# Transformer block on one core: query and output projections in five packed groups, fourteen score blocks a pass on VectorE

## Chip, core and metric

The kernel runs on one core of a Trainium2 chip. The metric is the device time of one execution in microseconds, and the median over runs. The core has five engines with a queue of instructions each, worked off in order: TensorE (PE, with its weight loads PEld), VectorE (DVE), ScalarE (ACT), GpSimd (POOL) and SyncE (SP), which here issues most DMAs. Results of TensorE lie in PSUM, eight banks of 512 f32 values on each of 128 partitions; everything else lies in SBUF.

## What is computed

A transformer block before normalisation: attention of 32 query heads with one shared key and value head of width 20, then a gated FFN, each with a residual. S = 2048 tokens, D = 640, Df = 1536, bf16.

```python
x = A_x
xn = layernorm(x)
q = (xn @ wq).reshape(B, S, 32, 20).transpose(0, 2, 1, 3)
k, v = xn @ wk, xn @ wv
p = softmax(einsum("bhqd,bkd->bhqk", q, k) * 20 ** -0.5)
h = x + einsum("bhqk,bkd->bhqd", p, v).transpose(0, 2, 1, 3).reshape(B, S, 640) @ wo
g, u = layernorm(h) @ w_gate, layernorm(h) @ w_up
out = h + (gelu(g) * u) @ w_down
```

## The kernel before

**Padded heads.** A head is 20 wide and takes 32 rows: four heads fill 128 partitions (rows 0 to 19, 32 to 51, 64 to 83, 96 to 115; the twelve rows after each are zero). 32 heads are NG = 8 groups. wq is widened into wq_pad (L323, L449, L462 to L465), wo into wo_pad (L327, cleared L1166, loaded by four DMAs L1169). q stands in qT (L331) in two slots of 512 tokens (a chunk), made by q_proj (L585): per chunk and group five matmuls over D, and one cast by VectorE (L608). The first chunk is made by q_proj_first (tile 0) and a q_proj over tiles 1 to 3.

**Attention in blocks.** There are 16 tiles of 128 tokens with two halves each, four groups (16 heads) to a half; a tile's half is a pass. A pass has 64 blocks (16 key tiles x 4 head rows). For a block one matmul (qk_mm, L665) on 32 rows gives 128 keys by 512 scores; four blocks on different rows run side by side. Five blocks make a cycle: three in banks 0 to 2, two in banks 3 and 4, and ACT takes the exponential of each set in one instruction (L743) into one of three buffers pbuf. PV (L811) multiplies each block with the values on 32 columns, four heads side by side, into one bank that collects the pass.

**Blocks on VectorE.** Some blocks of a pass (D_UNITS = 12; the first pass none, the last two D_LAST = 8) are not given to ACT: stream_d (L669) puts their scores into an aux bank, VectorE writes them as integers (L699), which read as bf16 approximate a power of two, and shifts two more copies per pair of blocks (L708); PV then takes three weighted terms of each such block (values v_w, scaled for the last ND_KT = 3 key tiles). With 12 such blocks a pass has 52 left for ACT.

**After a pass**, normalise (L830) transposes, divides and transposes back (L837, L842, L849) into onT. After both halves of a tile, wo_proj (L894) multiplies onT with wo_pad, eight matmuls of 512 columns and eight of 128 (L906), and VectorE adds to xh (L913). Then come the second layer norm, a transpose by DMA (L507), the FFN (L942 to L985, tanh on ACT L975), its down projection (L1001) and the store (L1012). The last tile has its own function (last_tile, L1016).

**Order.** A planner in the code (_Sched, L41 to L276) gives each task a duration, dependences, a priority and slots of buffers, plays them through (schedule, L94) and so fixes the order on every engine; semaphore waits (resolve, L225) keep it correct. Score matmuls of the stream go ahead of other TensorE tasks when these would delay them by more than a spare time (L140 to L152). A DMA holds SP's queue for 0.08 us in the plan and ends after its given duration (L187); a task waiting for it adds HOP (0.12 for SP) and its lag (0.3 for side work on TensorE). Side work is what is neither scores nor PV: projections and FFN. It shares two aux banks (5 and 7, AUX_pool) with the scores of VectorE's blocks.

A second plan in the program, "with_maximum", runs only if a sum of the softmax falls outside a range; it doesn't run here.

Of the kernel before, what the change touches and what calls it, by code (L numbers as in the profile page):

```python
# [10 lines left out]
P = 128  # L11
# [13 lines left out]
class _Pool:  # L25
    def __init__(self, n):
        self.free_at = [0.0] * n
        self.users = [[] for _ in range(n)]
        self.busy = [False] * n

# [4 lines left out]
class _Task:  # L35
    __slots__ = ("eng", "fn", "dur", "deps", "prio", "acq", "rel", "dma", "name", "start", "end", "seq",
                 "extra", "sem", "val", "needed", "know", "pos", "lag", "cfg", "after", "paced", "opens", "rides",
                 "groups", "late", "spare")


class _Sched:  # L41
# [13 lines left out]
    SPARE_A, SPARE_B = .28, .7  # L55

# [10 lines left out]
    def add(self, eng, fn, dur, deps=(), prio=0.0, acq=(), rel=(), dma=None, name="", lag=0.0,  # L67
# [7 lines left out]
        t.spare = None  # L75
        t.after = list(after)
# [17 lines left out]
    def schedule(self):  # L94
# [8 lines left out]
        cfg = None  # L103
# [19 lines left out]
        while left:  # L123
            best = None
            for e in self.ENGINES:
                cands = []
                for at, t in ready[e]:
                    if t.rides and not (cfg == t.cfg and at <= free[e] + 0.02 and t.rides() - groups):
                        at += self.PATIENCE
                    if t.paced and paced:  # L130
                        at = max(at, paced_at - self.AHEAD)
                    for s in t.acq:
                        p = s.pool
                        open_ = [f for f, b in zip(p.free_at, p.busy) if not b]
                        if not open_:
                            break
                        at = max(at, min(open_))
                    else:
                        cands.append((max(at, free[e]), t))
# [16 lines left out]
                pick = min((c for c in cands if c[0] <= t0 + 1e-9), key=lambda c: (c[1].prio, c[1].seq))  # L156
# [5 lines left out]
            if e == "pe" and opened is not None and not (t.cfg is None and at - free[e] < self.GAP):  # L162
# [11 lines left out]
            for s in t.acq:  # L174
# [3 lines left out]
                p.busy[i] = True  # L178
                t.extra += p.users[i]
# [9 lines left out]
            else:  # L189
# [16 lines left out]
                if e == "pe" and t.cfg is None:  # L206
                    whole = t.end
                    paced_at = max(paced_at, at) + dur / self.SHARE
# [70 lines left out]
def bass_sequential_preLN__grouped_kv_mqa__glu_gated_geglu__prompt_kernel(  # L279
# [31 lines left out]

    sc = _Sched()
# [10 lines left out]
    wq_pad = sb("wq_pad", [P, ND, H, 32])  # L323
# [3 lines left out]
    wo_pad = sb("wo_pad", [P, NG, D])  # L327
# [32 lines left out]
    ND_KT = 3  # L360
    v_w = sb("v_w", [P, 3, ND_KT, 32])
    wq_sb = dbuf[:].rearrange("p a b n -> p (a b n)")[:, 0:ND * D].rearrange("p (c n) -> p c n", c=ND)
# [86 lines left out]
    z_wq = sc.add("pool", lambda e: e.memset(wq_pad[:, :, :, Dh:32], 0.0), 2.0, prio=nprio(), name="z_wq")  # L449
# [11 lines left out]
    for h in range(2):  # L461
        wq_c.append(sc.add("act", (lambda h: lambda e: e.activation(  # L462
            wq_pad[:, :, 16 * h:16 * h + 16, 0:Dh],
            wq_sb.rearrange("p c (h n) -> p c h n", h=H)[:, :, 16 * h:16 * h + 16, :], ACT.Copy))(h),
            d_act(1600), [dma_wq, z_wq], prio=nprio(), name=f"wqpad{h}"))  # L465

    def wq_l(cc, g):
        return wq_pad[:, cc, 4 * g:4 * g + 4, :].rearrange("p a b -> p (a b)")
# [90 lines left out]

    def q_proj_first(h, sl, bk, eng):  # L560
        pr = nprio()

        def part(g0):
            def fn(e):
                ins = None
                for g in range(g0, g0 + 2):
                    for cc in range(ND):
                        ins = e.matmul(bk()[:, g * P:(g + 1) * P], wq_l(cc, 4 * h + g),
# [3 lines left out]
        a = sc.add("pe", part(0), 0.65, ln1_T[0] + [wq_c[h]], prio=pr, acq=[sl], name=f"q0a_{h}")  # L572
        b = sc.add("pe", part(2), 0.65, [a], prio=pr, name=f"q0b_{h}")
        o = qT[:, 0, 4 * h:4 * h + 4, 0:P]

        def ev(e):
            i = bk().rearrange("p (g n) -> p g n", g=4)
            return e.activation(o, i, ACT.Copy) if eng == "act" else e.tensor_copy(o, i)
        q_ready[(0, h)] = [sc.add(eng, ev, d_act(512) if eng == "act" else d_ps(512), [b], prio=pr, rel=[sl],
                                  name=f"q0e_{h}")]  # L580
        xnT_readers[0].append(b)

    last_qk = {}

    def q_proj(c, g, t0, t1):  # L585
# [12 lines left out]
        deps = [x for t in range(t0, t1) for x in ln1_T[t]] + [wq_c[g // 4]] + xnT_readers[NT - 1][:1]  # L598
# [6 lines left out]
        for t in range(t0, t1):  # L605
            xnT_readers[t].append(d)
        o = qT[:, c % 2, g, (t0 % 4) * P:(t0 % 4) * P + n]
# [3 lines left out]
        for t in range(t0, t1):  # L611
            q_ready.setdefault((t, g // 4), []).append(ev)

# [7 lines left out]
    D_UNITS, D_LAST = 12, 8  # L621
# [38 lines left out]
    state = {"pv": None, "ont": None, "qk": None}  # L660
# [8 lines left out]
    def stream_d(n, which):  # L669
# [11 lines left out]
        def choose(task, used):  # L681
# [5 lines left out]
            if u[3] in used:  # L687
# [3 lines left out]
                      prio=HOT + 4 * n + (1 if which else 0.5), acq=[ax] + ([d_sl] if half == 0 else []),  # L691
                      name=f"qkd_{n}", cfg="row", rides=lambda: {u[3] for u in left})
        qk_t.late = choose
        last_qk[(t, h)] = qk_t
# [60 lines left out]
    def pv(n, t, h, part, exps, p_sl):  # L755
# [60 lines left out]
        pv_t.late = choose  # L816
        if n == in_pass[(t, h)][1]:
# [76 lines left out]
    def wo_proj(t, ont):  # L894
        deps0 = [onorm[(t, 0)], onorm[(t, 1)]] + wo_ready
        done = []
        for c0, c1 in ((0, 512), (512, D)):
# [3 lines left out]
            step = 1 if c0 == 0 else 4  # L901
            for g0 in range(0, NG, step):
                def fn(e, g0=g0, c0=c0, c1=c1, step=step, bk=bk):
                    ins = None
                    for g in range(g0, g0 + step):
                        ins = e.matmul(bk()[:, 0:c1 - c0], onT[:, ont.index, g, :], wo_pad[:, g, c0:c1],  # L906
                                       start=(g == 0), stop=(g == NG - 1))
                    return ins
                lastp = g0 + step == NG
                prev = sc.add("pe", fn, 0.215 if c0 == 0 else 0.2225, deps0 if prev is None else [prev], prio=pr,  # L910
# [8 lines left out]
    def ffn(t0, t1):  # L919
# [6 lines left out]
        for tri in range(NF // (3 * k)):  # L926
            gsl = G_pool.slot()
            ges, zts, uts, first_g = [], [], [], []
            for j in range(3):
# [26 lines left out]
                gm, pr = job(wg_sb, dma_wg, "g", acq + [ax], [], bk)  # L956
                ge = sc.add("dve", lambda e, gsl=gsl, col=col, bk=bk: e.tensor_copy(g_gs[:, gsl.index, col], bk()),  # L957
# [10 lines left out]
                um, pr = job(wu_sb, dma_wu, "u", [ax], [], bk)  # L968
                uts.append(sc.add("dve", lambda e, gsl=gsl, col=col, bk=bk: e.scalar_tensor_tensor(  # L969
# [10 lines left out]
            for j in range(3):  # L980
# [7 lines left out]
                    [ths[j], uts[j]], prio=pr, acq=acq, rel=[gsl], after=hh_all[:1], name=f"hh{t0}_{fc0}"))  # L988
# [26 lines left out]

    def last_tile(t, ont):  # L1016
# [15 lines left out]
        def wo_part(j, c0, c1, g0):  # L1032
            def fn(e):
                ins = None
                for g in range(g0, g0 + 4):
                    ins = e.matmul(acc(j), onT[:, ont.index, g, :], wo_pad[:, g, c0:c1], start=False, stop=(g == NG - 1))
# [3 lines left out]
        for j, c0, c1 in halves_:  # L1040
            r = add("pe", wo_part(j, c0, c1, 0), 0.56, [r, onorm[(t, 0)]] + wo_ready, name=f"wa{j}_{t}")
# [124 lines left out]
    z_wo = sc.add("pool", lambda e: e.memset(wo_pad[:], 0.0), 4.5, [ln1_nm[NT - 1]], prio=nprio(), name="z_wo")  # L1166
    wo_ready = []
    for hl in range(4):
        wo_ready.append(load("sp", wo_pad[32 * hl:32 * hl + Dh, :, :],  # L1169
                             A_wo.rearrange("(g l d) n -> l d g n", g=NG, l=4)[hl], f"wo{hl}", 6.0,  # L1170
                             [z_wo] + after_T))
# [10 lines left out]
    for t in range(NT):  # L1182
# [11 lines left out]
        if t % 4 == 0 and t + 4 < NT:  # L1194
# [3 lines left out]
            for g in range(NG):  # L1198
                q_proj(t // 4 + 1, g, t + 4, t + 8)
            counter[0] = max(keep, counter[0])  # L1200
        ffn(t, t + 1)

# [46 lines left out]
    with nc.body("with_maximum"):  # L1249
# [6 lines left out]
        wo_ready, outs = [], []  # L1256
# [37 lines left out]
        for t in range(NT):  # L1294
# [5 lines left out]
            for h in range(2):  # L1300
                ax, bk = aux()

                def q_all(e, h=h, t=t, bk=bk):
                    ins = None
                    for g in range(4):
                        for cc in range(ND):
                            ins = e.matmul(bk()[:, g * P:(g + 1) * P], wq_l(cc, 4 * h + g),
# [4 lines left out]
                q_done.append(sc.add("dve", lambda e, h=h, bk=bk: e.tensor_copy(  # L1312
                    qT[:, 0, 4 * h:4 * h + 4, 0:P], bk().rearrange("p (g n) -> p g n", g=4)), 0.7, [a], prio=nprio(),
                    rel=[ax], name=f"ge{t}_{h}"))
# [55 lines left out]
```

## Time and profile before

| | us |
|---|---|
| runs | 834.09, 835.21, 835.84 (median 835.21) |
| the profiled execution | 833.07 |
| its span, first to last instruction | 831.0 |
| first exponential (L743) starts | 14.6 |
| last exponential starts | 806.1 |
| landing of a transpose xnT<-xn_tmp, median | 2.6 |
| landing of a store out_dram<-xh, median | 1.8 |

Busy slices of the span, 40 equal ones, in tenths (9 is 90% or more):

```
PE   4898999999999999999999999999999999999997
DVE  7567878888788877987787798878888788777762
ACT  5899999999999999999999999999999999999991
POOL 6500001001001111011000011111101011011010
```

A matmul's listed time is its length from start to end; consecutive ones overlap, so the busy time of a group is less than count times length. Lines of a group read: line, engine, operation, out<-in with partitions x elements, xcount, then busy us, mean ns of one, and the engine's idle time before them with what ended it. Some matmul records are missing (L594 should have 120 of 512 columns, L906 120).

### The profile page before, as it was taken

The page shows a single profiled execution, that of the slowest core. Times are in us where ns is not written, and L with a number is a line of the kernel's source. Part 1 is how long each engine was busy: PE and PEld are TensorE (multiplying, and loading weights), DVE is VectorE, ACT ScalarE, POOL GpSimd, SP SyncE. Part 2 cuts the span into 40 slices and gives each one's busy share as a digit, 9 for nine tenths or more (in the row PEclk, how much of TensorE's full clock was granted, in tenths as well). Part 3 has the DMA queues.
Part 4 walks back from the last instruction along what each step waited for, and adds up shares of the span by engine and source line. Part 5 has one row for each costly group of instructions (what it writes and reads, how often), then busy time and mean ns, then how long its engine had stood idle before and what let it go on. Part 6 is the DMA issues. An engine that isn't in the chain of part 4 may idle for free.

```text
span 831.0 us, 17917 instructions
## 1 busy us (share of the span) xinstructions
PE 767.0 (92%) x7743; PEld 303.9 (37%) x7800; DVE 648.7 (78%) x1320; ACT 799.6 (96%) x740; POOL 92.4 (11%) x157
## 2 busy tenths in 40 slices
PE   4898999999999999999999999999999999999997
PEld 3322233333234343333323343343434333334345
DVE  7567878888788877987787798878888788777762
ACT  5899999999999999999999999999999999999991
POOL 6500001001001111011000011111101011011010
PEclk9899999999999999999999999999999999999999
DMA  8680000000000000000000000000000000000000
GB/s 215 113 285 1 10 1 9 1 10 9 1 9 10 9 9 2 17 2 17 1 9 10 1 10 9 9 9 10 10 1 17 9 9 2 17 2 9 17 1 20
DMA packets 30347, 18.94 MB, mean 23 GB/s; under 512 B 21944, under 2 KB 28984, under 8 KB 30264
## 3 DMA queue, kind: packets, MB, share of 16 engines
q1 hardware_dynamic: 28808, 17.54, 8.2%
q8 instruction: 62, 1.02, 0.5%
q10 hardware_dynamic: 1456, 0.22, 0.2%
q14 instruction: 21, 0.17, 0.1%
HBM read 10.21 MB, written 2.62 MB: 15 GB/s over the span
## 4 chain that ended last, share of the span: by engine, by line
ACT 85%; PE 9%; DVE 4%; DMA 1%; issue 0%; SPq 0%
ACT pbuf L743 83%; PE ps L665 3%; ACT g_z L975 2%; PE ps L811 2%; PE ps L942 1%; DVE dbuf L699 1%; PE ps L1106 1%; DVE dbuf L708 1%; PE ps L1001 1%; DMA xh<-in_A_x_dram 1%; DVE hhT L985 1%; DMA xnT<-xn_tmp 1%; PE ps L1115 0%; ACT kT L551 0%; PE ps L906 0%
## 5 line engine op out<-in xcount | busy, mean ns | idle before, releaser
L743 ACT ACTIVATE pbuf<-ps 128x1536 bf16<-128x1536 f32 (+1 forms) x674 | 766.8, 1334 | 4.4 <-PE ps L665 4.0
L665 PE MATMUL ps<-qT,kT 32*128 32x512 bf16 x2048 | 289.0, 386 | 38.4 <-ACT pbuf L743 24.8
L699 DVE TENSOR_SCALAR dbuf<-ps 128x512 int16<-128x512 f32 x364 | 247.0, 683 | 88.2 <-PE ps L665 85.8
L811 PE MATMUL ps<-pbuf,v_ext 128*32 128x512 bf16 x1684 | 210.4, 389 | 1.0 <-DVE oT L837 0.5
L811 PE MATMUL ps<-dbuf,v_w 128*32 128x512 bf16 x1092 | 161.2, 380 | 0.0
L665 PEld LDWEIGHTS ps<-qT,kT 32*128 32x128 bf16 x2048 | 73.8, 91 | 226.9 <-ACT pbuf L743 165.7
L708 DVE TENSOR_SCALAR dbuf<-dbuf 128x1024 int16<-128x1024 int16 x364 | 145.2, 433 | 2.7
L960 POOL TENSOR_TENSOR g_z<-g_gs 128x512 bf16<-128x512 bf16 x45 | 49.2, 1092 | 423.6 <-DVE g_gs L957 423.6
L942 PE MATMUL ps<-xnT,wg_sb 128*128 128x128 bf16 x900 | 69.6, 220 | 2.6 <-DVE dbuf L699 1.8
L811 PEld LDWEIGHTS ps<-pbuf,v_ext 128*32 128x32 bf16 x1684 | 40.6, 93 | 82.8 <-issue 68.1
L942 PE MATMUL ps<-xnT,wu_sb 128*128 128x128 bf16 x900 | 69.6, 220 | 0.8 <-DVE dbuf L699 0.4
L1001 PE MATMUL ps<-wd_sb,hhT 128*128 128x128 bf16 (+1 forms) x335 | 62.8, 296 | 2.4 <-issue 1.4
L942 PEld LDWEIGHTS ps<-xnT,wg_sb 128*128 128x128 bf16 x900 | 50.8, 98 | 35.4 <-issue 21.7
L942 PEld LDWEIGHTS ps<-xnT,wu_sb 128*128 128x128 bf16 x900 | 50.8, 98 | 33.7 <-issue 22.8
L811 PEld LDWEIGHTS ps<-dbuf,v_w 128*32 128x32 bf16 x1092 | 45.7, 96 | 14.1 <-issue 2.5
L594 PE MATMUL ps<-xnT,wq_pad 128*128 128x512 bf16 (+1 forms) x143 | 42.9, 370 | 1.5 <-issue 0.6
L906 PE MATMUL ps<-wo_pad,onT 128*128 128x128 bf16 (+1 forms) x225 | 42.4, 297 | 1.7 <-issue 1.4
L1001 PEld LDWEIGHTS ps<-wd_sb,hhT 128*128 128x128 bf16 x360 | 22.9, 97 | 42.0 <-issue 30.7
L483 POOL CAST lnvb<-mv 128x1 bf16<-128x1 f32 x31 | 6.1, 198 | 270.4 <-DVE mv L481 270.4
L957 DVE CAST g_gs<-ps 128x512 bf16<-128x512 f32 x45 | 30.6, 681 | 7.0 <-PE ps L942 6.6
L963 DVE SCALAR_TENSOR_TENSOR g_z<-g_z,g_gs 128x512 bf16<-128x512 bf16 x45 | 30.6, 680 | 5.5 <-POOL g_z L960 5.5
L969 DVE SCALAR_TENSOR_TENSOR g_us<-ps,g_gs 128x512 bf16<-128x512 f32 x45 | 30.6, 680 | 4.4 <-PE ps L942 4.3
(96 smaller groups left out, 407.8 us busy)
## 6 DMA issues: line engine op xcount, KB each, us to landing
out_dram<-xh SPq DMA_DIRECT2D x15, 160.0 KB, 1.8
xh<-in_A_x_dram SPq DMA_DIRECT2D x3, 640.0 KB, 8.6
wg_sb<-in_B_w_gate_dram SPq DMA_DIRECT2D x1, 1920.0 KB, 7.8
wu_sb<-in_B_w_up_dram SPq DMA_DIRECT2D x1, 1920.0 KB, 12.3
wd_sb<-in_B_w_down_dram SPq DMA_DIRECT2D x1, 1920.0 KB, 19.2
dbuf<-in_A_wq_dram SPq DMA_DIRECT2D x1, 800.0 KB, 5.2
wo_pad<-in_A_wo_dram SPq DMA_DIRECT2D x4, 200.0 KB
xnT<-xn_tmp SPq DMA_TRANSPOSE x30, 2.6
```

Of the source, the lines that this page charges most:

```text
L594: ins = e.matmul(bk()[:, 0:n], wq_l(cc, g), xnT[:, cc, t0 * P:t1 * P], start=(cc == 0), stop=(cc == ND - 1))
L665: return e.matmul(bk.rearrange("p (g n) -> p g n", g=4), kT4[r, kt * P:(kt + 1) * P], qT[r, (t // 4) % 2, 4 * h:4 * h + 4, (t % 4) * P:(t ...
L699: bits = sc.add("dve", lambda e: e.tensor_scalar(buf(0, w), bk(), D_BIAS, 0.0, ALU.add, ALU.max), 0.61, [qk_t] + wq_c, prio=HOT + 100, rel ...
L708: "dve", lambda e, j=j: e.tensor_scalar(buf(j), buf(0), D_SHIFT[j], None, ALU.add), 0.335,
L743: exps.append(sc.add("act", lambda e, w0=w0, w1=w1: e.activation(pbuf[:, p_sl.index, w0:w1], ps[:, w0:w1], ACT.Exp, scale=EXP_SCALE), (1.3 ...
L811: ins = e.matmul(ps[32 * hl:32 * hl + 32, PVB * 512:(PVB + 1) * 512], v, ap(), start=start, stop=stop, tile_position=(0, 32 * hl))
L906: ins = e.matmul(bk()[:, 0:c1 - c0], onT[:, ont.index, g, :], wo_pad[:, g, c0:c1], start=(g == 0), stop=(g == NG - 1))
L942: ins = e.matmul(bk()[:, f * n:(f + 1) * n], wsb[:, cc, (fc0 + f) * P:(fc0 + f + 1) * P], xnT[:, cc, tok], start=(cc == 0), stop=(cc == ND ...
L957: ge = sc.add("dve", lambda e, gsl=gsl, col=col, bk=bk: e.tensor_copy(g_gs[:, gsl.index, col], bk()), d_ps(512), [gm], prio=EVAC + pr, rel ...
L960: sqt = sc.add("pool", lambda e, gsl=gsl, col=col: e.tensor_tensor(g_z[:, gsl.index, col], g_gs[:, gsl.index, col], g_gs[:, gsl.index, col ...
L963: zt = sc.add("dve", lambda e, gsl=gsl, col=col: e.scalar_tensor_tensor(g_z[:, gsl.index, col], g_z[:, gsl.index, col], GELU_K, g_gs[:, gs ...
L1001: ins = e.matmul(bk()[:, 0:c1 - c0], hhT[:, hh.index, fc, tl], wd_sb[:, fc, c0:c1], start=(fc == 0), stop=(fc == NF - 1))
```

## The change

- **Packing.** Five groups of 128 columns (NC = 5) take all 32 heads: heads of groups 0 to 4 stay on their rows, and the twelve heads of groups 5 to 7 are cut into pieces that lie in the twelve free rows behind each head (PIECES). wq_pk and wo_pk have that order.
- **q.** For chunks 1 to 3, q_proj runs over five groups; then 16 DMAs (q_pieces) copy the pieces from SBUF to SBUF into groups 5 to 7 of qT, whose other rows are cleared once by GpSimd (z_qT). The first chunk keeps eight groups, with groups 5 to 7 of wq in wq_x, which borrows the space of hhT. wq_pk is filled by ACT (two copies, and a third for wq_x) and GpSimd (four copies).
- **Output.** For tiles 0 to 14, once both halves are normalised, 16 DMAs copy the pieces of onT from groups 5 to 7 into the free rows of groups 0 to 4; wo_proj then has five matmuls of 512 columns and five of 128. wo_pk is loaded by 4 + 16 DMAs, with no clear before, ahead of the FFN weights. The last tile keeps eight groups with a padded wo_tail in the space of xnT, cleared by four GpSimd instructions and loaded by 16 DMAs after tile 10's FFN tasks.
- **Blocks.** D_UNITS 14, D_LAST 10, v_w for four key tiles. A pass then has 50 blocks for ACT, ten cycles.
- **Order.** A PV task that is not a pass's last gives way to side work until the scores are BACKLOG = 5 turns past it (yields); when a VectorE block's scores are DUE = 2 turns overdue, other tasks may not take an aux bank while side work holds one (due); the scores of such blocks keep an order (after).

```diff
+    BACKLOG, BEHIND = 5, 1e7
+    DUE = 2
...
+                due = e == "pe" and any(t.due is not None and t.due + self.DUE <= turn and not any(
+                    all(s.pool.busy) and not any(s.pool.side) for s in t.acq) for _, t in ready[e])
...
-                        if not open_:
+                        if not open_ or due and t.due is None and any(b and d for b, d in zip(p.busy, p.side)):
...
-                pick = min((c for c in cands if c[0] <= t0 + 1e-9), key=lambda c: (c[1].prio, c[1].seq))
+                yields = e == "pe" and turn - min((t.yields for _, t in ready[e] if t.yields is not None), default=turn) < self.BACKLOG
+                pick = min((c for c in cands if c[0] <= t0 + 1e-9), key=lambda c: (
+                    self.BEHIND if yields and c[1].yields is not None else c[1].prio, c[1].seq))
...
+    NC = D // P
+    PIECES = ((0, 3, 0, 12, 5, 0), (3, 2, 0, 8, 5, 12), (3, 1, 8, 4, 7, 12), (4, 1, 8, 4, 7, 16))
+    def pieces():
+        for c, k, r, n, g, d0 in PIECES:
+            for l in range(4):
+                yield (slice(32 * l + Dh + r, 32 * l + Dh + r + n), slice(c, c + k),
+                       slice(32 * l + d0, 32 * l + d0 + n), slice(g, g + k))
...
-    ND_KT = 3
+    ND_KT = 4
...
+    z_qT = sc.add("pool", lambda e: e.memset(qT[:, 1, NC:NG, :], 0.0), 1.0, [x_ready[NT - 1]], prio=nprio() + 40, name="z_qT")
...
+    for c, k, r, n, g, d0 in PIECES:
+        wq_c.append(sc.add("pool", lambda e, c=c, k=k, r=r, n=n, g=g, d0=d0: e.tensor_copy(
+            wq_v[:, :, 4 * c:4 * c + 4 * k, Dh + r:Dh + r + n], wq_n[:, :, 4 * g:4 * g + 4 * k, d0:d0 + n]),
+            0.1 + n * k / 45.0, [dma_wq], prio=nprio(), name=f"wqp{c}_{r}"))
...
+    def q_pieces(slot, n0, n1, deps, name):
+        pr = nprio()
+        return [sc.add("sp", lambda e, x=x: e.dma_start(qT[x[2], slot, x[3], n0:n1], qT[x[0], slot, x[1], n0:n1]),
+                       2.0, deps, prio=pr, dma=f"d_{name}", name=f"{name}p") for x in pieces()]
...
+        if c and g == NC - 1:
+            moved = q_pieces(c % 2, 0, n, q_ready[(t0, 0)] + q_ready[(t0, 1)] + [z_qT] * (c == 1), f"q{c}")
+            for t in range(t0, t1):
+                q_ready[(t, 1)] += moved
...
-    D_UNITS, D_LAST = 12, 8
+    D_UNITS, D_LAST = 14, 10
...
+        qk_t.due = 2 * n + which
...
+        if not last:
+            pv_t.yields = 2 * n
...
-        deps0 = [onorm[(t, 0)], onorm[(t, 1)]] + wo_ready
+        pr = nprio()
+        deps0 = [sc.add("sp", lambda e, x=x: e.dma_start(onT[x[0], ont.index, x[1], :], onT[x[2], ont.index, x[3], :]),
+                        2.0, [onorm[(t, 0)], onorm[(t, 1)]], prio=pr, dma=f"d_op{t % 2}", name=f"op{t}") for x in pieces()]
+        deps0 += [onorm[(t, 0)], onorm[(t, 1)]] + wo_ready
...
-            step = 1 if c0 == 0 else 4
-            for g0 in range(0, NG, step):
+            step = 1 if c0 == 0 else NC
+            for g0 in range(0, NC, step):
...
+    LT = 10
+    wo_tail = xnT[:, 0:4, 0:LT * P].rearrange("p c (g n) -> p c g n", g=2)
+    def load_tail():
+        free_ = [x for t in range(LT) for x in ffn_read[t]]
+        z = [sc.add("pool", lambda e, c=c: e.memset(wo_tail[:, c, :, :], 0.0), 0.8, free_, prio=nprio(), name=f"z_wt{c}")
+             for c in range(4)]
+        return [load("sp", wo_tail[32 * l:32 * l + Dh, c, :, :], wo_n[l, :, 2 * c:2 * c + 2, :], "wt", 6.0, z)
+                for l in range(4) for c in range(4)]
...
-    z_wo = sc.add("pool", lambda e: e.memset(wo_pad[:], 0.0), 4.5, [ln1_nm[NT - 1]], prio=nprio(), name="z_wo")
...
+    for l in range(4):
+        wo_ready.append(load("sp", wo_pk[32 * l:32 * l + Dh, :, :], wo_n[l, :, 0:NC, :], "wo", 6.0, after_T))
+    for i, (p0, c, p1, g) in enumerate(pieces()):
+        l, d0 = i % 4, p1.start % 32
+        wo_ready.append(load("sp", wo_pk[p0, c, :], wo_n[l, d0:d0 + p1.stop - p1.start, g, :], "wo", 6.0, after_T))
...
-            for g in range(NG):
+            for g in range(NC):
                 q_proj(t // 4 + 1, g, t + 4, t + 8)
```

## Prediction

> **What bounds the kernel now.** First the page: busy times, then the chain that ended last.
>
> ```profile
> span 831.0 us, 17917 instructions
> PE 767.0 (92%) x7743; PEld 303.9 (37%) x7800; DVE 648.7 (78%) x1320; ACT 799.6 (96%) x740; POOL 92.4 (11%) x157
> ...
> ACT 85%; PE 9%; DVE 4%; DMA 1%; issue 0%; SPq 0%
> ```
>
> ScalarE (ACT) is busy 96% and carries 85% of the chain. Next the groups with shapes kept apart, for prices, and one window over the regular part, 100 to 800 us, taken whole and for L743 alone.
>
> ```profile
> L743 ACT ACTIVATE pbuf<-ps 128x1536 bf16<-128x1536 f32 x337 | 520.9, 1546 | 2.9 <-PE ps L665 2.6
> L743 ACT ACTIVATE pbuf<-ps 128x1024 bf16<-128x1024 f32 x336 | 377.9, 1125 | 1.5 <-PE ps L665 1.4
> L699 DVE TENSOR_SCALAR dbuf<-ps 128x512 int16<-128x512 f32 x364 | 247.0, 683 | 88.2 <-PE ps L665 85.8
> L708 DVE TENSOR_SCALAR dbuf<-dbuf 128x1024 int16<-128x1024 int16 x364 | 145.2, 433 | 2.7
> L906 PE MATMUL ps<-wo_pad,onT 128*128 128x512 bf16 x105 | 33.5, 384 | 1.7 <-issue 1.4 <-DVE g_us L969 0.2
> L594 PE MATMUL ps<-xnT,wq_pad 128*128 128x512 bf16 x103 | 32.9, 384 | 1.5 <-issue 0.6 <-DVE dbuf L708 0.3 <-DVE dbuf L699 0.2
> L608 DVE CAST qT<-ps 128x512 bf16<-128x512 f32 x24 | 16.2, 675 | 2.0 <-PE ps L594 1.5 <-PE ps L665 0.2 <-PE ps L811 0.2
> L906 PE MATMUL ps<-wo_pad,onT 128*128 128x128 bf16 x120 | 9.8, 220 | 0.0
> ```
>
> ```profile
> 100.00:800.00 700.00, 662.94 (x6771) 258.74 (x6821) 569.44 (x1115) 698.40 (x615) 64.06 (x87) 1.00 0.03 8
> ...
> 100.00:800.00 700.00, 681.38 (x601) 1.00 0.03 8
> ```
>
> In that window ACT idles 1.6 us in 700: every block of exponentials that leaves it is worth its whole time, as long as TensorE (37 us of gaps) and VectorE (131 us idle) follow. The window has 601 exponentials of 2.5 blocks on average, so 681.38/1502 = 0.4535 us a block.
>
> **The change, part by part.**
>
> *Blocks moved.* 29 passes hand over 14 instead of 12 and the last two 10 instead of 8: 62 blocks. ACT: 62 x 0.4535 = **-28.1 us**, on the path. VectorE: 62 x (247.0/364 + 145.2/364) = 62 x 1.078 = +66.8 us; three fewer casts of q for each of three later chunks, 9 x 0.675 = -6.1; net +60.7. In the window, about 58 of these on 569 make some 627 busy out of 672 left (45 idle). They lie beside ACT; without that cover they become the third rival. I charge 1 us of extra ACT waits (0 to 8).
>
> *TensorE.* Three of eight groups go, in 3 chunks x 5 matmuls of L594 (45 x 32.9/103 = 14.4 us) and in 15 tiles of L906 (45 x 33.5/105 = 14.4, and 45 x 9.8/120 = 3.7): -32.5. Each moved block turns one PV matmul into three, so +124, four side by side: 31 rounds of at most 0.38 us (the length of one), +11.8. The 62 extra score matmuls ride beside others for nothing or cost up to 0.39 each, 0 to +24. TensorE thus has 0 to 20 us less work while ACT gives up 28: gaps stay near today's, and I take nothing on the path.
>
> *PV behind side work, due blocks.* They reorder TensorE's static queue and add no instruction; ACT waited for it only 4 us in all, so the gain is bounded at 4 and I take 0; a loss lies in the rivals.
>
> *The packed rows.* q: 16 small DMAs from SBUF to SBUF per chunk, three chunks, 48. Their product is read four tiles later, over 100 us; hidden. The output side is different: each of fifteen tiles now has 16 DMAs between the last transpose of its normalised output (L849) and its first output matmul (L906), 240 in all, on SP's queue. TensorE runs a fixed order, so if the matmul comes up before the DMAs land, all behind it wait: the next scores first, and then ACT. SP and its landings show the prices:
>
> ```profile
> L1012 SPq DMA_DIRECT2D out_dram<-xh x15: 332/332/387, 168.2 to 812.4; - x15
> ...
> DMA to landing us min/median/max: 1.8/1.8/2.1
> ```
>
> ```profile
> 37.59 0.39 SPq L427 DMA_DIRECT2D wg_sb<-in_B_w_gate_dram  x1
> 38.02 0.53 SPq L427 DMA_DIRECT2D wu_sb<-in_B_w_up_dram  x1
> ```
>
> No such small copy is in this trace. An issue takes 0.33 us in the nearest row, with 0.04 before the next (37.98 to 38.02): 0.37 apart. Bounds: 0.30, the shortest of any here, and 0.58 (four x loads in 2.33 us at the start). Landing: 1.6 for the two halves of the last store (80 KB), 1.8 for a whole one; I take 1.6. The sixteenth lands 15 x 0.37 + 1.6 + 0.1 = 7.25 us after the transpose. The code's planner counts 0.08 for an issue, 2.0 for the DMA and 0.56 of hops: 0.14 + 1.2 + 2.0 + 0.42 = 3.76 us. So the DMAs are **3.5 us late** (with 0.30: 2.4; with 0.58 and 1.8: 6.8).
>
> What covers this is how long the planner lets the matmul stand once it is ready, because no PSUM bank is free or scores go first. Before, it was ready 0.44 us after the transpose. In the timeline of tile 0:
>
> ```profile
> 79.00 0.70 DVE L849 STREAM_TRANSPOSE onT<-oN 128x512 bf16<-128x512 bf16 x1
> ...
> 80.46 0.38 PE L906 MATMUL ps<-wo_pad,onT 128*128 128x512 bf16 x1
> ```
>
> It ends at 79.70; L906 starts 0.76 later. The other tiles, read the same way: 5.63, 1.37, 3.42, 2.27, 5.16, 1.29, 1.72, 7.20, 4.36, 1.94, 4.34, 4.14, 1.97, 3.04. Less 0.44 this is a stand of 0.3 to 6.8. With the same stands after the change, TensorE waits 3.5 less each, where positive: 3.2, 2.6, 0.5, 1.7, 2.7, 2.2, 2.0, 2.0 and 0.9, and six tiles nothing; 17.8 us. ACT meanwhile has a group in hand, up to 1.1 us (the 1024-wide row); I take 0.9 off each. That leaves 2.3 + 1.7 + 0.8 + 1.8 + 1.3 + 1.1 + 1.1 = **+10 us** (0 if all stands exceed the lateness; 15 x 2.6 = 39 if none helps).
>
> [...] The landings above are all stores to HBM; the copies stay in SBUF. [...] No run here shows a landing in SBUF but the transposes' 2.6 us. [...]
>
> *Start.* Filling the free rows of wq adds four GpSimd copies, 1200 elements a partition; by the L449 memset (1.7 us for 1920, 0.9 ns each) about 1.1, by L960 (1.09 for 512, 2.1 ns) 2.6. They become ready as the wq load lands at 6.39, just where GpSimd works on tile 1's layer norm:
>
> ```profile
> 6.74 0.23 POOL L483 CAST lnvb<-mv 128x1 bf16<-128x1 f32 x1 [0.93 <-DVE mv L481]
> ```
>
> Tile 1's transpose at 9.11 ends on the chain, so it can slip by up to 2.6; ACT's three copies keep their 3200 elements. I take **+1 us** (-1 if the first scores are put ahead of tile 1's keys, to +2.6). The clear of wq's side has the same 1920 elements; the clear of wo (4.4 us, off the path) goes; twenty wo loads ahead of the FFN weights delay these by about 20 x 0.37 = 7 us, while their first use follows tile 0's attention, after 92 us.
>
> *Last tile.* It keeps eight groups, from a padded copy loaded by 16 DMAs after four clears on GpSimd, around tile 10; over 150 us of cover. SP holds them some 6 us, so a tile's pieces behind them could be late once. Zero, bounds 0 to 6.
>
> **Sum**, against the profiled execution, 833.07 us (span 831.0): 833.07 - 28.1 + 10 + 1 + 1 = 817.0. The median shown, 835.21, stands 2.1 above that execution, so a median of **819 us**.
>
> **Rivals.**
>
> 1. *All DMAs covered.* For it: landings in SBUF may be quicker, and a busier VectorE makes banks scarcer, so stands grow. Against: seven tiles before stood under 2 us. 835.2 - 28.1 = 807.
>
> 2. *The pieces stop TensorE in each tile; slower.* Place: the first L906 after L849. Side work now goes ahead of PV, so the matmul may come up as soon as the planner thinks it ready. Then ACT loses 3.5 - 0.9 = 2.6 us in each of 15 tiles, 39: 835.2 - 28.1 + 39 + 2 = 848. It decides from 28.1/15 = 1.9 us of ACT loss a tile. Against: only one of fifteen first matmuls came within half a microsecond of being ready.
>
> 3. *VectorE becomes the bound.* It waits in order, mostly in front of L699:
>
> ```profile
> DVE dbuf L699 <- PE ps L665: 73.3, 101, 1.8
> ```
>
> That is 73.3 of the window's 131 idle. Only 45 can remain. If half of the 131 are waits that cannot be shed, the kernel runs 66 - 45 = 21 us over: 835.2 - 28.1 + 21 + 1 = 829; two thirds would bring 850. Against: VectorE waits because scores are paced by ACT, so such waits should shrink as work fills them.
>
> A difference under 0.2%, 1.7 us, cannot be told from no change here.
>
> **Chances.** Forecast (about 811 to 824) 0.42; rival 1 (803 to 810) 0.22; rival 2 (835 and up) 0.18; rival 3 (824 to 840) 0.18. Faster than 833.5: 0.42 + 0.22 + 0.13 of rival 3 = 0.77; within 0.2%: 0.04; slower: 0.19. The range 803 to 838 leaves out 0.03 below and some 0.14 above; the forecast's own is 811 to 824.
>
> **What would show it.** L743 near 650 executions, 1622 blocks, and still nearly all of ACT's middle. On SP, sixteen issues 0.3 to 0.4 us apart per tile, the last landing about 7 us after L849. In the waits, the output matmul's line waiting for a DMA into onT, some 18 us over up to nine tiles, and ACT idle before L743 near 15 where it was 4. VectorE near 709 us, TensorE 745 to 770. The prediction is wrong if onT waits are near zero (then 807), if they come in all fifteen tiles (rival 2), or if ACT's new idle follows score matmuls held by L699 (rival 3).

## The result and the profile after

The changed kernel takes 957.23 us (median of 4 runs, 954.25 to 959.79) where the kernel before takes 834.65: ratio 1.1466, 95% interval 1.1424 to 1.1507. 819 with a range of 803 to 838 was forecast. The second rival had named the place; its price, 848, was also far too low.

The page of the changed kernel, busy times and the chain that ended last (new line numbers: L806 is the exponential, L724 scores, L874 PV, L963 the output's pieces, L976 the output projection, L762 VectorE's blocks):

```profile
span 956.8 us, 18504 instructions
PE 801.4 (84%) x7849; PEld 309.6 (32%) x7849; DVE 694.3 (73%) x1435; ACT 780.4 (82%) x716; POOL 95.5 (10%) x165
...
PE 36%; ACT 28%; DVE 16%; SPq 15%; DMA 3%; issue 2%; POOL 0%; DVEq 0%
ACT pbuf L806 27%; SPq L963 13%; PE ps L724 11%; PE ps L874 10%; DVE dbuf L762 6%; PE ps L1012 5%; PE ps L976 4%; DVE dbuf L771 3%; PE ps L1073 3%; DMA onT<-onT 2%; DVE hhT L1057 1%; DVE oT L903 1%; PE ps L1291 1%; SPq L602 1%; DVE onT L915 1%
```

ACT falls from 85% of the chain to 28%, and SP's queue, whose share before rounds to 0%, has 15%: issuing the pieces (L963) is itself on the chain. The waits, longest first (engine, line, who was waited for, us in total, times, longest):

```profile
DVE dbuf L762 <- PE ps L724: 154.2, 97, 18.0
ACT pbuf L806 <- PE ps L724: 147.3, 66, 17.6
...
PE ps L976 <- DMA onT<-onT: 111.1, 14, 17.3
...
PEld ps L976 <- DMA onT<-onT: 25.2, 3, 8.6
```

TensorE stands in front of the output projection until the pieces land; ACT, which waited 4.0 us for scores before, now waits 147.3. The stops sum to 111 us in fourteen tiles; the weight loads' 25.2 us lie beside them and are not to be added. One tile shows how. SP's issues by line (ns min, median, max), then the timelines of VectorE and TensorE, and of ACT, at tile 2:

```profile
L963 SPq DMA_DIRECT2D onT<-onT x240: 584/618/891, 81.9 to 885.7; - x120
```

```profile
192.70 0.70 DVE L915 STREAM_TRANSPOSE onT<-oN 128x512 bf16<-128x512 bf16 x1
...
198.54 0.38 PE L874 MATMUL ps<-dbuf,v_w 128*32 128x512 bf16 x1
205.38 1.01 PE L976 MATMUL ps<-wo_pk,onT 128*128 128x512 bf16 x2 [6.47 <-DMA onT<-onT]
206.33 0.60 PE L724 MATMUL ps<-qT,kT 32*128 32x512 bf16 x1
```

```profile
198.52 2.57 ACT L806 ACTIVATE pbuf<-ps 128x1536 bf16<-128x1536 f32 x2
208.49 2.36 ACT L806 ACTIVATE pbuf<-ps 128x1536 bf16<-128x1536 f32 x2 [7.40 <-PE ps L724]
```

The transpose ends at 193.40. Sixteen issues follow, 0.62 us the median and 0.05 apart, until 204.2; the matmul starts at 205.38, 1.2 us later and 11.98 after the transpose. It is much the same in the other tiles: 11.9 to 12.4 us in fourteen of fifteen. The plan has it ready 3.76 after, so it is **8.2 us late**. In tile 7 it comes 21.6 us after, because a chunk of q sends its own sixteen pieces first:

```profile
473.20 11.13 SPq L602 DMA_DIRECT2D qT<-qT  x16
484.38 10.76 SPq L963 DMA_DIRECT2D onT<-onT  x16
```

And after each of the fourteen stops TensorE runs slower: over the next 5 us its granted clock is 0.50 to 0.63. Windows at tile 2, before, during and after the stop (us, then busy us of PE, PEld, DVE, ACT, POOL, then the granted clock, the DMA engines' share and GB/s), and one window inside the slow stretch:

```profile
180.00:199.00 19.00, 18.89 (x226) 8.54 (x224) 16.40 (x33) 19.00 (x18) 2.08 (x2) 1.00 0.02 5
199.00:205.40 6.40, 0.01 (x1) 0.05 (x2) 1.30 (x3) 2.09 (x2) 0.00 (x0) 0.70 0.01 3
205.40:215.00 9.60, 9.60 (x48) 1.85 (x48) 5.28 (x10) 5.32 (x5) 0.00 (x0) 0.66 0.00 0
206.00:211.00 5.00, 5.00 (x21) 0.81 (x20) 3.25 (x6) 2.36 (x2) 0.00 (x0) 0.50 0.00 0
```

A score matmul takes 0.60 us behind the stop where it took 0.39. The mean clock is 0.91; if all of the shortfall is at the 0.50 of this stretch, that is (1 - 0.91) x 2 x 956.8 = 172 us at half clock.

### The profile page after: what moved, and what is told of

It reads as the page before. It is cut to its first block, busy times and chain, and to the rows that moved or that the text cites. A ratio compares the mean times of both kernels' runs of the same rounds, so it can differ in the third digit from the quotient of the medians.

```text
span 956.8 us, 18504 instructions
## 1 busy us (share of the span) xinstructions
PE 801.4 (84%) x7849; PEld 309.6 (32%) x7849; DVE 694.3 (73%) x1435; ACT 780.4 (82%) x716; POOL 95.5 (10%) x165
## 4 chain that ended last, share of the span: by engine, by line
PE 36%; ACT 28%; DVE 16%; SPq 15%; DMA 3%; issue 2%; POOL 0%; DVEq 0%
ACT pbuf L806 27%; SPq L963 13%; PE ps L724 11%; PE ps L874 10%; DVE dbuf L762 6%; PE ps L1012 5%; PE ps L976 4%; DVE dbuf L771 3%; PE ps L1073 3%; DMA onT<-onT 2%; DVE hhT L1057 1%; DVE oT L903 1%; PE ps L1291 1%; SPq L602 1%; DVE onT L915 1%
## 5 line engine op out<-in xcount | busy, mean ns | idle before, releaser
L806 ACT ACTIVATE pbuf<-ps 128x1536 bf16<-128x1536 f32 (+1 forms) x649 | 747.5, 1295 | 148.9 <-PE ps L724 147.3
L762 DVE TENSOR_SCALAR dbuf<-ps 128x512 int16<-128x512 f32 x426 | 285.7, 682 | 156.2 <-PE ps L724 154.2
L724 PE MATMUL ps<-qT,kT 32*128 32x512 bf16 x2048 | 290.1, 400 | 22.8 <-ACT pbuf L806 12.4
L874 PE MATMUL ps<-pbuf,v_ext 128*32 128x512 bf16 x1622 | 212.4, 403 | 1.1 <-ACT pbuf L806 0.6
L874 PE MATMUL ps<-dbuf,v_w 128*32 128x512 bf16 x1278 | 175.9, 398 | 0.6 <-DVE oT L903 0.6
L771 DVE TENSOR_SCALAR dbuf<-dbuf 128x1024 int16<-128x1024 int16 x426 | 169.4, 432 | 1.9
L724 PEld LDWEIGHTS ps<-qT,kT 32*128 32x128 bf16 x2048 | 72.2, 91 | 236.1 <-ACT pbuf L806 139.8
L976 PE MATMUL ps<-wo_pk,onT 128*128 128x512 bf16 (+1 forms) x150 | 44.2, 425 | 111.5 <-DMA onT<-onT 111.1
L1012 PE MATMUL ps<-xnT,wu_sb 128*128 128x128 bf16 x900 | 69.7, 222 | 0.6 <-DVE dbuf L762 0.4
L1012 PE MATMUL ps<-xnT,wg_sb 128*128 128x128 bf16 x900 | 67.6, 221 | 1.5 <-DVE dbuf L771 1.1
L1073 PE MATMUL ps<-wd_sb,hhT 128*128 128x512 bf16 (+1 forms) x360 | 66.8, 303 | 0.7 <-DVE xh L1081 0.5
L874 PEld LDWEIGHTS ps<-pbuf,v_ext 128*32 128x32 bf16 x1622 | 40.2, 94 | 82.6 <-issue 68.3
L1012 PEld LDWEIGHTS ps<-xnT,wu_sb 128*128 128x128 bf16 x900 | 51.3, 98 | 30.5 <-issue 17.7
L1012 PEld LDWEIGHTS ps<-xnT,wg_sb 128*128 128x128 bf16 x900 | 51.2, 98 | 26.7 <-issue 15.8
L874 PEld LDWEIGHTS ps<-dbuf,v_w 128*32 128x32 bf16 x1278 | 50.7, 98 | 24.3 <-DVE oT L903 4.6
L976 PEld LDWEIGHTS ps<-wo_pk,onT 128*128 128x128 bf16 x150 | 12.6, 115 | 135.3 <-issue 106.8
L983 DVE TENSOR_TENSOR xh<-xh,ps 128x512 bf16<-128x512 bf16 (+1 forms) x30 | 14.3, 484 | 55.2 <-PE ps L976 55.1
L1291 PE MATMUL ps<-halves,zeros 128*128 128x512 bf16 x89 | 35.4, 400 | 0.0
L1073 PEld LDWEIGHTS ps<-wd_sb,hhT 128*128 128x128 bf16 x360 | 23.6, 97 | 34.3 <-issue 20.7
```

Of the source, the lines that this page charges most:

```text
L724: return e.matmul(bk.rearrange("p (g n) -> p g n", g=4), kT4[r, kt * P:(kt + 1) * P], qT[r, (t // 4) % 2, 4 * h:4 * h + 4, (t % 4) * P:(t ...
L762: bits = sc.add("dve", lambda e: e.tensor_scalar(buf(0, w), bk(), D_BIAS, 0.0, ALU.add, ALU.max), 0.61, [qk_t] + wq_c, prio=HOT + 100, rel ...
L771: "dve", lambda e, j=j: e.tensor_scalar(buf(j), buf(0), D_SHIFT[j], None, ALU.add), 0.335,
L806: exps.append(sc.add("act", lambda e, w0=w0, w1=w1: e.activation(pbuf[:, p_sl.index, w0:w1], ps[:, w0:w1], ACT.Exp, scale=EXP_SCALE), (1.3 ...
L874: ins = e.matmul(ps[32 * hl:32 * hl + 32, PVB * 512:(PVB + 1) * 512], v, ap(), start=start, stop=stop, tile_position=(0, 32 * hl))
L1012: ins = e.matmul(bk()[:, f * n:(f + 1) * n], wsb[:, cc, (fc0 + f) * P:(fc0 + f + 1) * P], xnT[:, cc, tok], start=(cc == 0), stop=(cc == ND ...
```

## The experiments

All compare with the kernel before on the same chip, 834.7 to 835.2 us in these sets. The two columns on the right are of the profiled execution. e4 is not in the table: its copies were timed one by one (834.15 us in its single run).

| run | us | ratio to before (95%) | last exponential ends, us | tail after it, us |
|---|---|---|---|---|
| before | 834.65 | | 806.7 | 24.3 |
| changed | 957.23 | 1.1466 (1.1424 to 1.1507) | 930.1 | 26.6 |
| e1 issue counted | 820.89 | 0.9831 (0.9808 to 0.9854) | 786.2 | 32.0 |
| e2 output unpacked | 828.90 | 0.9929 (0.9907 to 0.9952) | 784.4 | 43.3 |
| e3 order and blocks | 838.45 | 1.0043 (1.0025 to 1.0061) | 781.3 | 55.3 |
| e5 fewer fillers | 820.64 | 0.9843 (0.9819 to 0.9867) | 783.9 | 34.1 |
| e6 PV not behind | 843.40 | 1.0098 (1.0081 to 1.0115) | 783.4 | 59.0 |
| e7 twelve blocks | 839.62 | 1.0058 (1.0041 to 1.0074) | 812.0 | 25.1 |
| e8 thirteen blocks | 822.09 | 0.9852 (0.9836 to 0.9869) | 792.8 | 27.7 |
| e9 lateness 4 us | 867.57 | 1.0386 (1.0366 to 1.0406) | 831.3 | 34.5 |
| e10 tile 14 unpacked | 820.81 | 0.9830 (0.9813 to 0.9846) | 786.0 | 33.6 |
| e11 the same, fewer fillers | 821.37 | 0.9853 (0.9828 to 0.9877) | 783.3 | 34.3 |
| e12 warm wait | 938.17 | 1.1227 (1.1198 to 1.1256) | 910.1 | 26.5 |

**e1: one number of the planner.**

```diff
-                free[e] = at + 0.08
+                free[e] = at + (0.675 if t.dma[:4] in ("d_op", "d_q1", "d_q2", "d_q3") else 0.08)
```

> The changed kernel, with one number of its planner altered: a piece's DMA holds SP's queue for 0.675 us in the plan instead of 0.08, as the trace of the changed kernel shows them (0.58 to 0.78 us an issue, 0.05 between). Nothing is added or taken away. Theory A (the loss is the plan's alone: the output matmul stands 8 us too early in TensorE's order): the wait of the output matmul for onT<-onT falls from 136 us to under 5, ACT's wait for scores from 147 us to under 15, the clock is back at 0.99, and the time is 806 to 820 us. Theory B (VectorE or TensorE cannot follow at fourteen blocks a pass, and the wait only hides it): ACT still waits 25 us or more for scores, and the time is 830 us or more.

Measured 820.89 us. The chip's DMAs are the same; the output matmuls now come 11.9 to 24.9 us after the transpose, none stopped for more than 0.2. (The 136 us of the expectation add the weight loads' 25.2 to the 111 of the matmul.) Its waits:

```profile
DVE dbuf L762 <- PE ps L724: 66.3, 96, 9.2
...
ACT pbuf L806 <- PE ps L724: 7.9, 20, 1.1
```

ACT's wait for scores is gone but for 7.9 us. So the whole loss of the changed kernel, 957.23 - 820.89 = 136 us, hangs on this one number, by which the plan places the output projection, and theory A holds. 820.89 is just above its range, and the table says why: the last exponential ends 20.5 us earlier than before, but the tail behind it is 7.7 us longer.

**e2: output projection as before, q packed.**

```diff
-        deps0 = [sc.add("sp", lambda e, x=x: e.dma_start(onT[...], onT[...]), ...) for x in pieces()]
+        deps0 = []
-            for g0 in range(0, NC, step):
+            for g0 in range(0, NG, step):
...
+                acq=[hh] if i == 0 else [], rel=[u_sl] + ([gsl] if i == 2 else []), after=hhs[:1], ...))
```

(wo is loaded by four DMAs after a clear, as before, and the last tile reads it; the last line keeps the last tile's three products in order.)

> The changed kernel with the output projection as before (eight groups, four loads, no pieces; q stays packed). TensorE has 18 us more to do than in the changed kernel. Theory A (the 240 output pieces are the loss): no wait for onT, clock 0.99, 806 to 822 us. Theory B (TensorE needs the packed output projection to hold fourteen blocks): 830 us or more, with ACT waiting for scores behind side work.

Measured 828.90 us: between the two theories. No wait for pieces, yet 8.0 us slower than e1, and all of that is tail: 43.3 us against 32.0, with the last exponential 1.8 us earlier.

**e3: order and blocks, nothing packed.** The kernel before with the planner's new rules, D_UNITS 14, D_LAST 10 and four key tiles of v_w.

> The kernel before with the order's edits (yields, due, after) and the fourteen blocks alone; no packing at all, so TensorE keeps the 32 us that the packing takes off and gets 12 us more of PV. Theory A (ACT alone sets the pace, TensorE has room): 806 to 815 us. Theory B (the packing is what makes room): ACT waits for scores 15 us or more, and the time is 820 to 850 us.

Measured 838.45 us, 0.4% slower than before: the time that theory B gave, without the sign that it named. ACT waits 6.5 us for scores, not 15, and its last exponential ends at 781.3, 25.4 us earlier than before. But the tail is 55.3 us. What lies there is FFN of earlier tiles. The window behind the last exponential, matmuls of the gate and up projections alone (L942 before, L1012 in e1, L961 in e3; busy PE, PEld, clock, DMA share, GB/s); the three lines are of the kernel before, e1 and e3:

```profile
806.80:831.00 24.20, 0.00 (x0) 0.00 (x0) 0.95 0.06 17
```

```profile
786.30:818.20 31.90, 4.42 (x70) 4.13 (x70) 0.98 0.06 18
```

```profile
781.30:836.50 55.20, 18.49 (x310) 17.79 (x310) 0.98 0.05 17
```

A tile has 120 of them. Before, none is left when ACT ends; in e1 0.6 of a tile, in e2 1.7 (208), in e3 2.6. TensorE gives ACT its scores first and leaves side work for the end: its shortage shows as a longer tail, not as waits of ACT. The shortage is of time that the plan can fill. From 100 to 780 us TensorE (the first busy time) idles 36.6 us before, 25.7 in e1 and 21.9 in e3, never zero:

```profile
100.00:780.00 680.00, 643.43 (x6539) 249.30 (x6590) 554.11 (x1087) 678.40 (x598) 60.93 (x84) 1.00 0.03 8
```

```profile
100.00:780.00 680.00, 654.33 (x6743) 252.45 (x6740) 604.72 (x1210) 674.86 (x591) 68.91 (x91) 1.00 0.05 11
```

```profile
100.00:780.00 680.00, 658.12 (x6629) 248.50 (x6630) 599.18 (x1195) 676.20 (x593) 57.13 (x79) 1.00 0.04 8
```

More than half of what is left (14.0 us in e1, 12.3 in e3) stands in front of scores whose banks ACT has not freed. Whether the two aux banks, which side work shares with the scores of VectorE's blocks, hold side work back as well was not tested.

**e4: the price of a copy.** On the kernel before, sixteen copies in a row on SP, each waiting for the last:

```diff
+        if t == 3 and ident is not None and t_zeros is not None:
+            d = onorm[(t, 1)]
+            for k, (n, to) in enumerate(probes):      # n = 128, 16, 12, 4 partitions
+                for _ in range(4):
+                    d = sc.add("sp", lambda e, n=n, to=to: e.dma_start(to[0:n, :], xnT[0:n, 0, 0:P]), 2.0, [d], ...)
```

> The kernel before, with sixteen copies of 256 B rows from SBUF to SBUF on SP's queue after tile 3's attention, each waiting for the one before: four each of 128, 16, 12 and 4 partitions. Theory A (an issue costs more where the partitions are not a multiple of sixteen): 0.33 us for 128 and 16, 0.55 to 0.7 for 12 and 4. Theory B (any copy inside SBUF costs about 0.6 to issue): 0.6 for all four. Landing 1.0 to 1.8 us after the issue in both. The time of the whole is not the point.

The timeline of SP, one copy of each size, in the order 128, 16, 12, 4 partitions:

```profile
228.74 0.47 SPq L922 DMA_DIRECT2D to<-xnT  x1
...
237.42 0.51 SPq L922 DMA_DIRECT2D to<-xnT  x1
...
247.62 0.71 SPq L922 DMA_DIRECT2D to<-xnT  x1
...
256.41 0.58 SPq L922 DMA_DIRECT2D to<-xnT  x1
```

Both theories miss a part. A copy inside SBUF costs 0.47 us to issue where the store from as many partitions took 0.33; twelve partitions cost 0.71, 0.2 more than sixteen, though there are fewer. In the changed kernel the output's pieces of twelve partitions take 0.71 to 0.78 (once 0.89), with three rows of 256 B a partition where the copy here has one; those of eight 0.62 to 0.66, of four 0.58 to 0.61. The copies of 128 and 16 partitions land 1.7 us (1.6 to 2.5) after the issue starts. For 12 and 4 the trace has no landing, but each copy waits for the one before, and within a set these follow one another after 1.6 to 1.9 us, one pair after 2.9.

**e5: fewer fillers.** e1 with `OVERDUE` 5.0 instead of 2.0. A filler is a matmul with zeros that the planner puts in and that adds nothing to the result.

> As e1, with the planner's limit on time without a full-array matmul, after which it puts in a filler (OVERDUE), at 5.0 us instead of 2.0. In e1 there are 82 fillers (31.8 us of TensorE) where the kernel before has 29 (11.7 us), and the tail after the last exponential is 32.0 us where it was 24.3. Theory A (TensorE is short of time in e1, and the fillers are part of it): fillers under 35, the tail 24 to 29 us, and 808 to 817 us in all. Theory B (the fillers hold the clock): the granted clock falls under 0.98, and the time is 822 us or more. If TensorE is not short, the time stays at 818 to 823 with fewer fillers.

Measured 820.64 us, e1 within noise, neither theory's time; only 16 of 82 fillers went (66 left), and the clock is 0.994. ACT ends 2.3 us earlier than in e1, the tail is 2.1 longer. So these 16 were not what TensorE lacked; whether the 37 that remain beyond the 29 of before cost anything was not shown.

**e6: PV not behind side work.** e1 with `pv_t.yields = None`.

> As e1, without the part that puts PV behind side work (no task yields); due and the order of VectorE's blocks stay. Theory A (that part brings side work forward, so the tail is shorter with it): the tail grows past 36 us, and the time is 825 to 845 us. Theory B (it only spreads side work unevenly and calls for fillers): fillers fall to about 30, and the time is 808 to 818 us.

Measured 843.40 us: theory A. The tail grows to 59.0 us, with 310 gate and up matmuls in it. This part of the change is worth 22.5 us beside the others. How it gains is seen only in part: in e6 TensorE is busy 781.5 us over the whole, in e1 767.5, though e6 has 14 fillers fewer and the projections, the FFN and the blocks are the same. In the order of e6 the same work takes more of TensorE's time; a little of that is the clock, 0.988 against 0.993.

**e7 and e8: twelve and thirteen blocks.** e1 with D_UNITS, D_LAST = 12, 8 and 13, 9.

> As e1, with twelve blocks a pass and eight in the last two, as before: packing and order alone. ACT then has the 28 us of exponentials back, TensorE has 18 us or more to spare. Theory A (the blocks are what pays, the packing only makes room): last exponential near 807 to 810 us, tail near 24, 831 to 836 us in all. Theory B (the packing pays by itself through a shorter tail or start): under 828 us.

> As e1, with thirteen blocks a pass and nine in the last two. Theory A (at fourteen TensorE is the bound, at twelve ACT; the best lies between): the last exponential near 795, tail 24 to 28 us, 814 to 821 us, the same as e1 or a little under. Theory B (ACT alone sets it): half of the step from e7 to e1, about 826 us.

e7 measured 839.62 us, 4.5 above before: packing and order pay nothing without blocks, and it is 3.6 us over even theory A, with the last exponential at 812.0 instead of 806.7. Of these 5 us, 4.4 are waits of ACT for scores (8.4 where it had 4.0); why they grew was not tested. e8 measured 822.09, 1.1 us over theory A's range and 4 under theory B: ACT ends 6.6 us later than in e1, the tail is 4.3 shorter. Between thirteen and fourteen blocks ACT's gain and TensorE's tail nearly balance.

**e9: lateness of 4 us.** e1 with 0.37 in the place of 0.675: the prediction's own price for an issue, given to the plan.

> As e1, but the planner counts 0.37 us for a piece, the price that the prediction took, where the chip takes 0.675: the plan has the pieces landed 8.1 us after the transpose, the chip 12.0, so each output matmul is planned about 3.9 us early (3.5 in the prediction). Theory P (as predicted: the matmul stands 0.3 to 6.8 us in the plan after it is ready, and ACT has 0.9 us in hand): waits for onT of some 20 us over nine tiles, ACT loses 10 to 14, 830 to 836 us. Theory Q (with PV behind side work it stands nowhere, and what follows a stop runs at a lower clock): waits in twelve tiles or more, 45 us or more in all, and 855 us or more.

Measured 867.57 us, 46.7 over e1. The waits:

```profile
ACT pbuf L806 <- PE ps L724: 50.1, 50, 3.8
...
PE ps L976 <- DMA onT<-onT: 20.6, 8, 3.5
PE ps L724 <- DMA onT<-onT: 12.6, 4, 4.7
```

The time is theory Q's, the waits lie between: 33 us in twelve tiles, where P had some 20 in nine and Q 45 in twelve or more. The last line belongs to them: a score does not read onT, but 15 of the 150 matmul records of L976 are missing in this trace, and where the first of a tile is, the score behind it shows the wait (and the missing matmul's own time in it, so 33 is a little too much). ACT loses 42 more than in e1, not 10 to 14, and the clock is 0.961, by the sum above 68 us at half clock against e1's 11. A stop costs ACT more than its length: 42 us for 33 here, 139 for 111 in the changed kernel.

**e10 and e11: tile 14 unpacked.** e1, and e5, with tile 14 taking the last tile's padded wo:

```diff
-            step = 1 if c0 == 0 else NC
-            for g0 in range(0, NC, step):
+            ng, wo_g = (NC, lambda g: wo_pk[:, g]) if t < 14 or not wo_ready else (NG, lambda g: wo_tail[:, g // 2, g % 2])
+            step = 1 if c0 == 0 else ng
+            for g0 in range(0, ng, step):
```

> As e1, with tile 14's output projection from the padded copy that the last tile reads (eight groups, no pieces); tiles 0 to 13 keep the pieces. In e1 tile 14's first output matmul comes 19.9 us after its transpose and 27 us before the last exponential, where the kernel before had 3.0 and 44. Theory A (its pieces push its FFN into the tail): the tail falls from 32.0 to 24 to 28 us, 812 to 817 us. Theory B (the tail holds what TensorE could not do before, whatever tile it belongs to): tail 31 us or more, 819 to 823 us.

> As e10, with the fillers' limit at 5.0 us as in e5. Theory A: as e10 within 2 us, since e5 took 16 fillers out and changed nothing. Theory B (with tile 14's latency gone, TensorE's time counts): 3 us or more under e10.

820.81 and 821.37 us: nothing gained, tails 33.6 and 34.3, with 60 and 72 gate and up matmuls. e10 is theory B: the tail holds what TensorE did not get done before, whatever tile it belongs to, not what tile 14's pieces delayed. e11 is theory A, e10 within 2 us.

**e12: warm wait.** The changed kernel; in front of the wait for the pieces TensorE multiplies zeros into the bank that it is about to fill.

```diff
+                    prev.warm = lambda e, bk=bk: [e.matmul(bk(), zeros[:], halves[:].unsqueeze(1).to_broadcast(
+                        [P, 4, P]), start=True, stop=True) for _ in range(28)]
```

> The changed kernel (planner as it is, 0.08 us a piece), with 28 matmuls of zeros, 6.0 us at full clock, in the bank of the output projection ahead of its wait for the pieces; they are no part of the result, and the plan doesn't count them. The stop in front of the output matmul is 6.1 to 8.3 us in twelve tiles, 17.3, 3.4 and 0.4 in three; so the pieces come no later for them, but for some 8 us in two tiles. Theory C (part of the loss is the lower clock after each stop, 174 us of it in all): the clock stays near 0.98, ACT's wait for scores falls from 147 to 100 to 120 us, and the time is 915 to 935 us. Theory D (the loss is the length of the stops alone): ACT's wait stays at 145 or more, and the time is 950 to 968 us.

Measured 938.17 us, 19 us less, between the theories' ranges; clock 0.982, ACT's wait 129.4. Tile 2 again, the window behind the stop:

```profile
205.40:215.00 9.60, 9.48 (x87) 2.63 (x86) 7.66 (x16) 9.60 (x9) 0.00 (x0) 1.00 0.00 0
```

87 matmuls instead of 48 in the same 9.6 us, and ACT is busy throughout where it had 5.32. So about 19 of the 136 us are the lower clock, and some more, since the zeros hold up two tiles: the output matmul comes 14.6 us after the transpose in tile 3 and 17.9 in tile 9, where it came 12.0 and 12.3. The rest goes with the stops.

## Why the prediction was wrong

- **Blocks moved, -28.1 us.** Right in count (1622 blocks, 649 exponentials) and nearly in size: once the stops are out, ACT is busy 741.8 us at L806 instead of 766.8, and its last exponential ends 20.5 (e1) to 25.4 us (e3) earlier.
- **The packed rows on the output side, +10 us: the step that failed.** Its sum was (late - stand - 0.9) over the tiles. *Late* was 3.5 us, and is 8.2: the price of an issue, 0.37, came from stores of 128 partitions to HBM, with the start's 0.58 as upper bound; pieces of 12, 8 and 4 partitions inside SBUF take 0.71, 0.64 and 0.58, some 0.68 apart on average. The landing, 1.6, was about right: the matmul starts 1.8 us after the last issue does. With 8.2 no stand of before (0.3 to 6.8) is long enough, and the *stand* did not stay: the matmul's start, less its stop, less 3.76, leaves under 1 us in ten of fifteen tiles, where three were under 1 before. So fourteen tiles stop, for 111 us, where nine were counted for 17.8; only in tile 9 the matmul came up with its pieces landed. And the *0.9 in hand* had the wrong sign: in e9, with a lateness near the predicted one, twelve tiles stop for some 33 us, and that costs 46.7. The granted clock falls to 0.50 behind most of these stops (the run's mean is 0.961, e1's 0.993), and ACT loses 42 us more than in e1 for the 33 of the stops. Even with lateness right, the time would have been out of the range. The upper end of the range took 2.6 us a tile; the prediction's own bound for lateness, 6.8, with no stand would have made it 15 x (6.8 - 0.9) = 88 us.
- **Rival 2** had the place and the mechanism, and the point from which it decides: 1.9 us of ACT's loss a tile; measured (147.3 - 4.0)/15 = 9.6. Its chance of 0.18 rested on the row of the cheap store and on the stands of before.
- **q's pieces, hidden.** Right for q, wrong for SP's queue: in tile 7 they stand ahead of the output's pieces, whose matmul comes 9.6 us later than in the other tiles. The step counted who reads the product, not who is queued behind it.
- **TensorE, nothing on the path.** Wrong by 7.7 us in e1, the longer tail. The step looked at gaps; side work that finds no gap moves to the end. Output packing is worth 8.0 us (e2 to e1) and q's packing 9.5 (e3 to e2), both through a shorter tail: 43.3 to 32.0 and 55.3 to 43.3, while ACT ends 1.8 and 3.1 later.
- **PV behind side work, 0.** Worth 22.5 us (e6). It was bounded by ACT's waits, which it hardly touches (9.6 us in e6, 7.9 in e1); it shortens the tail. And "add no instruction" was wrong: with the new order the planner puts in 72 fillers in the place of 29 even where nothing is packed (e3), 82 in e1 and 89 in the changed kernel.
- **VectorE, rival 3.** Refuted: busy 694 us in the changed kernel and 697 in e1 (709 predicted), and its wait for scores is 66.3 us in e1, down from 85.8 (for L699) before, though it has 62 blocks more. The waits shrank as work filled them, as the prediction argued.
- **Start, +1 us.** Not resolved. In e1 the first exponential starts at 15.25 instead of 14.61, the 27th at 52.52 instead of 51.03; but in e4, whose start is that of the kernel before, they start at 14.87 and 52.44.
- **Landing, 1.6 us.** It came from stores, and rival 1 held that landings in SBUF may be quicker. The runs don't bear that out: the copies of e4 land after 1.6 us at the least, where the two halves of the last store took 1.6 and whole stores 1.8. The trace of before had other landings in SBUF than the transposes' 2.6 us: a load of 160 KB of x took 2.6 us too.

With the plan's one number mended the kernel takes 820.89 us, 1.7% under before, 2 us from the forecast. That is luck, errors that cancel: the stops of +10 us are not there, ACT ends 20.5 us earlier and not 28.1, and the tail is 7.7 longer.

## What to carry to other kernels

Where a fixed order is planned ahead, a wrong duration costs little while it hides, and about its full size in every repetition once work that feeds the busiest engine waits for it (8.2 us in fifteen tiles are 123 us, and 136 were lost): before a DMA is put in front of such an engine, measure issue and landing of that very shape, sixteen in a row, on the queue that will carry them. When a kernel gives its stream priority, look for lack of time not only in the stream's waits but in what is left when the stream ends.

## What the runs showed of the hardware

How long a copy's issue held SP differed with its partitions, and not in their order: 0.47 us for 128, 0.51 for 16, 0.71 for 12 and 0.58 for 4 (e4, one copy of each; all sixteen lie between 0.47 and 0.84). What in the issue takes longer for 12 and 4 partitions was not shown.

In tile 2 of the changed kernel, TensorE's granted clock was 0.66 over the 9.6 us behind a stop of 6.47 us, and 1.00 over the same 9.6 us where matmuls of zeros filled the stop (e12). Behind the shortest of the fourteen stops, 3.35 us in tile 3, it was 0.50 over the next 5 us; behind an idle 0.40 us in tile 9 it was 1.00. In e9 shorter stops than 3.35 us were followed by 0.50 too. The windows behind e9's stops in tiles 2 (2.63 us) and 6 (2.81 us):

```profile
185.30:192.00 6.70, 6.17 (x69) 2.55 (x68) 5.43 (x12) 5.14 (x6) 0.00 (x0) 1.00 0.01 2
388.40:395.00 6.60, 6.60 (x46) 2.72 (x44) 4.30 (x10) 4.50 (x4) 0.00 (x0) 0.50 0.01 4
```

In e9 the clock stayed at 1.00 behind stops of 0.7, 1.5, 1.6 and 2.6 us, and fell to 0.50 behind those of 2.8 us and more. One shown as 1.9 us (tile 11, whose first output matmul has no record) was followed by 0.50 as well, so no sharp limit is shown.
